# Windowed attention and a gated network: attention from split fp32r products on the full array to plain fp32 products on parts of it

## The chip, the core and the metric

The kernel runs on one core of a Trainium2 chip. The metric is the device time of one execution in microseconds (us), as the median of the runs. TensorE multiplies (its weight loads are listed apart as PEld), VectorE (DVE), ScalarE (ACT) and GpSimd (POOL) work on the memory beside it, and SyncE (SP) issues the copies, which 16 DMA engines carry out.

## The reference

There are 8 batches with 8 heads of width 64. Each batch has 512 local tokens and 32 global ones. A local query sees the 32 global keys and the local keys at a distance of at most 32; a global query sees all 544. All tokens then go through a network with a gate.

```python
s_g = scale * np.matmul(q_g, k_all.transpose(0, 1, 3, 2))
out_g = np.matmul(sm(s_g), v_all)
s_ll = scale * np.matmul(q_l, k_l.transpose(0, 1, 3, 2))
mask = np.abs(pos[:, None] - pos[None, :]) <= window      # window = 32
s_ll = np.where(mask, s_ll, -1000000000.0)
s_lg = scale * np.matmul(q_l, k_g.transpose(0, 1, 3, 2))
a_l = sm(np.concatenate([s_lg, s_ll], axis=-1))
out_l = np.matmul(a_l, np.concatenate([v_g, v_l], axis=2))
...
h = (x @ w1) * (x @ w2) @ w3        # x: 4352 x 512, w1, w2: 512 x 1024, w3: 1024 x 1024
return h @ w_out                     # w_out: 1024 x 512
```

## The kernel before

**The network.** `fold` multiplies w3 with w_out once, at the start, in plain fp32 (64 products of 512 columns). Weights come as 64-bit floats and are brought to fp32 on VectorE and ScalarE (`unit`). Every fp32 number of the network is then held as two fp32r parts, hi and lo, and a product is three: hi x hi, hi x lo, lo x hi. The tokens are cut into 17 keys: 16 half batches of 256 local tokens, and one key of all 256 global ones. A key has four quarters; in a quarter `first` makes 48 products of 256 columns (lines 780 to 782), the gate is multiplied on VectorE, and `second` makes 12 of 512 columns (lines 810 to 812). The gate of a quarter is worked on while TensorE is at the next one.

**Attention.** It goes by heads, and by pairs of heads (32 pairs) where both halves of the partitions are filled. A block has 128 queries and a window of 192 or 256 keys, so a head's scores are four steps (`scores`, line 513). In the first batch (heads under `FS`, `FV` = 8) these are plain fp32 products with 64 rows of contraction (line 506, values at 631 and 634). From the second batch on, keys are stored twice on the partitions (`both_k`, by copies from memory to memory on chip, `KO` and `KE`), so that one product of 128 rows holds q_hi and q_lo against the same keys. VectorE adds the mask and finds the maximum (line 517), ScalarE takes the exponential with its sum (line 521). The weights are turned so that keys stand on partitions: by TensorE's transposes up to head 11, and from head 12 (`FROM`) on by VectorE in blocks of 32 x 32 (line 546) and a way over DRAM (`pd`, then `RT` and `GR`). They are split into hi and lo (`PTh`, `PTl`), multiplied with values (lines 637, 642), and two halves are summed (`cb`, line 659). The inverse of a row's sum goes through DRAM (`rd`) to be laid over 64 partitions (`R`). The global queries of a pair have products of their own (line 691) and transposes (line 730).

**The order.** `ORDER_OF` is a table with one number for each step and, where several engines could do it, a letter for the engine. `in_order` sorts the steps by it, and that is the order on every engine. Each engine works its queue in order; the Tile layer sets the waits between engines.

## Time and profile before

| what | us |
|---|---|
| median of 3 runs | 843.74 |
| lowest, highest | 843.1, 844.06 |
| span of the profiled execution, first to last instruction | 839.6 |
| what lies around it, median of the runs less that span | 4.1 |
| TensorE busy in the span | 822.8 |
| VectorE busy | 669.5 |
| ScalarE busy | 436.8 |
| GpSimd busy | 318.4 |

The profile is of one execution; its own time is given as the span alone. Busy times of TensorE rest on modelled ends, so starts are the better guide there. A record is one line of the trace; several records can belong to one instruction of the program.

### The profile page before, as it was taken

The page shows a single profiled execution, that of the slowest core. Times are in us where ns is not written, and L with a number is a line of the kernel's source. Part 1 is how long each engine was busy: PE and PEld are TensorE (multiplying, and loading weights), DVE is VectorE, ACT ScalarE, POOL GpSimd, SP SyncE. Part 2 cuts the span into 40 slices and gives each one's busy share as a digit, 9 for nine tenths or more (in the row PEclk, how much of TensorE's full clock was granted, in tenths as well). Part 3 has the DMA queues.
Part 4 walks back from the last instruction along what each step waited for, and adds up shares of the span by engine and source line. Part 5 has one row for each costly group of instructions (what it writes and reads, how often), then busy time and mean ns, then how long its engine had stood idle before and what let it go on. Part 6 is the DMA issues. An engine that isn't in the chain of part 4 may idle for free.

```text
span 839.6 us, 17276 instructions
## 1 busy us (share of the span) xinstructions
PE 822.8 (98%) x5694; PEld 732.0 (87%) x5694; DVE 669.5 (80%) x1750; ACT 436.8 (52%) x1230; POOL 318.4 (38%) x465
## 2 busy tenths in 40 slices
PE   7999999799999999999999999999999999999998
PEld 5555469699999989999999999999999999999997
DVE  5878889998888888889898979987989878754343
ACT  5665667855455665467556645565655575400000
POOL 1133245454343634553343545546453555200000
PEclk8999999999999999999999999999999999999999
DMA  7777855566566676676776666667576575410000
GB/s 243 218 251 211 254 136 149 151 167 173 142 167 175 159 176 179 184 173 166 174 190 163 167 167 187 173 156 208 145 183 173 135 190 139 131 34 26 1 26 26
DMA packets 105921, 131.57 MB, mean 157 GB/s; under 512 B 29416, under 2 KB 64232, under 8 KB 105832
## 3 DMA queue, kind: packets, MB, share of 16 engines
q1 hardware_dynamic: 105832, 130.47, 58.5%
q8 instruction: 45, 0.74, 0.4%
q14 instruction: 44, 0.36, 0.2%
HBM read 76.38 MB, written 26.61 MB: 123 GB/s over the span
## 4 chain that ended last, share of the span: by engine, by line
PE 87%; DVE 7%; issue 2%; DMA 2%; ACT 1%; SPq 0%; POOL 0%; DVEq 0%; POOLq 0%; ACTq 0%
PE bp L780 7%; PE w L917 7%; PE bp L781 7%; PE bp L782 7%; PE acc L810 7%; PE ap L780 7%; PE acc L812 7%; PE acc L811 7%; PE ap L781 7%; PE ap L782 7%; PE s L513 5%; PE av L642 5%; PE sg L691 2%; PE av L637 2%; PE av L634 2%
## 5 line engine op out<-in xcount | busy, mean ns | idle before, releaser
L521 ACT ACTIVATE P<-P,mn 128x192 f32<-128x192 f32 (+1 forms) x256 | 121.4, 476 | 72.6 <-DVE mn L517 68.5
L780 PE MATMUL bp<-x,w12h 128*128 128x256 f32 x544 | 152.5, 280 | 1.2 <-DVE gl__8091 L418 1.0
L780 PE MATMUL ap<-x,w12h 128*128 128x256 f32 x544 | 153.0, 281 | 0.0
L781 PE MATMUL bp<-x,w12h 128*128 128x256 f32 x544 | 151.4, 278 | 0.0
L781 PE MATMUL ap<-x,w12h 128*128 128x256 f32 x544 | 151.3, 278 | 0.0
L782 PE MATMUL bp<-x,w12l 128*128 128x256 f32 x544 | 151.3, 278 | 0.0
L782 PE MATMUL ap<-x,w12l 128*128 128x256 f32 x544 | 151.3, 278 | 0.0
L780 PEld LDWEIGHTS bp<-x,w12h 128*128 128x128 f32 x544 | 102.5, 188 | 2.8 <-DVE gl__8091 L418 1.2
L781 PEld LDWEIGHTS ap<-x,w12h 128*128 128x128 f32 x544 | 102.6, 189 | 1.6 <-issue 0.2
L780 PEld LDWEIGHTS ap<-x,w12h 128*128 128x128 f32 x544 | 102.5, 188 | 1.6 <-issue 0.2
L781 PEld LDWEIGHTS bp<-x,w12h 128*128 128x128 f32 x544 | 102.6, 189 | 1.3
L782 PEld LDWEIGHTS ap<-x,w12l 128*128 128x128 f32 x544 | 102.3, 188 | 0.0
L782 PEld LDWEIGHTS bp<-x,w12l 128*128 128x128 f32 x544 | 102.3, 188 | 0.0
L517 DVE CUSTOM_DVE_ANT_0 P<-s,cs 128x192 f32<-128x192 f32 (+1 forms) x256 | 87.9, 385 | 12.4 <-PE s L513 7.6
L659 DVE TENSOR_TENSOR u<-av,cb 64x352 f32<-64x352 f32 x112 | 56.5, 518 | 6.5 <-ACT cb L415 4.6
L917 PE MATMUL w<-wo,w3f 128*128 128x512 f32 x128 | 61.1, 610 | 0.4 <-DVE wo L841 0.4
L415 ACT COPY cb<-av 64x352 f32<-64x352 f32 x95 | 41.7, 447 | 35.1 <-PE av L642 32.8
L546 DVE STREAM_TRANSPOSE P<-P 128x640 f32<-128x640 f32 x52 | 43.7, 841 | 19.0 <-ACT P L521 18.5
L642 PE MATMUL av<-PTl__1026,vs 128*128 128x192 f32 x224 | 55.9, 275 | 0.0
L642 PE MATMUL av<-PTh__1011,vs 128*128 128x192 f32 x224 | 54.5, 268 | 0.1
L521 ACT ACTIVATION_READ_ACCUMULATOR P<-P,mn 128x1 f32 x256 | 48.1, 188 | 0.0
L418 POOL TENSOR_TENSOR PTl__1026<-RT,PTh__1011 128x768 fp32r<-128x768 f32 x19 | 35.6, 1874 | 30.6 <-ACT PTh__1011 L415 15.2
(838 smaller groups left out, 2045.1 us busy)
## 6 DMA issues: line engine op xcount, KB each, us to landing
KO<-KE SPq DMA_DIRECT2D x56, 304.0 KB, 4.2
pd<-P SPq DMA_DIRECT2D x208, 80.0 KB, 2.3
RT<-pd SPq DMA_DIRECT2D x52, 256.0 KB, 3.3
raw_w<-in_w_t_dram SPq DMA_DIRECT2D x24, 512.0 KB, 4.6
kr<-in_kd_t_dram SPq DMA_DIRECT2D x32, 304.0 KB, 4.2
out_dram<-o SPq DMA_DIRECT2D x34, 256.0 KB, 2.6
KE<-KE SPq DMA_DIRECT2D x28, 304.0 KB, 3.3
qr<-in_q_t_dram SPq DMA_DIRECT2D x32, 256.0 KB, 3.7
```

The costliest lines, as they stand in the source:

```text
L517: nc.vector.tensor_tensor_reduce(blk(n, e), cut(n, T["st", n][:, e, 0 : WIN[e][1]]), cut(n, masks[e]), -0.125, 3.0e38, ALU.add, ALU.min, T ...
L521: nc.scalar.activation(blk(n, e), blk(n, e), AF.Exp, bias=T["mn", n][:, e : e + 1], scale=-1.0, accum_out=T["sm", n // 2][:, n % 2, e : e ...
L546: nc.vector.transpose(g[:, 1:6], g[:, 1:6])
L642: nc.tensor.matmul(av[:, o : o + c1 - c0], v, pt[:, j, c0:c1], start=False, stop=(j % 2 == y == 1), skip_group_check=True)
L659: nc.vector.tensor_add(T["u", n // 2][r : r + 64, x], T.pop(("av", n, x))[r : r + 64, 0:352], T["cb", n][r : r + 64, x])
L780: nc.tensor.matmul(d, wh[:, k, c, :], x[:, 0, 0:w], start=(k == m % 2 == 0), stop=False, skip_group_check=True)
L781: nc.tensor.matmul(d, wh[:, k, c, :], x[:, 1, 0:w], start=False, stop=False, skip_group_check=True)
L782: nc.tensor.matmul(d, wl[:, k, c, :], x[:, 0, 0:w], start=False, stop=(k == 3), skip_group_check=True)
L810: nc.tensor.matmul(a, gh[:, m % 2, sl], wh, start=(m == 0), stop=False)
L811: nc.tensor.matmul(a, gh[:, m % 2, sl], wl, start=False, stop=False)
L812: nc.tensor.matmul(a, gl[:, m % 2, sl], wh, start=False, stop=(m == 7))
L917: nc.tensor.matmul(T["w34", t], T["w3f", t, j // 4][:, j % 4], T["wo"][:, j], start=(j == 0), stop=(j == 7))
```

## The change

The network stays as it is: same products, same parts, same gate. Attention is written anew.

- No hi and lo parts of queries, keys, weights and values; products are plain fp32. Keys are not doubled; the sums `cb` and the inverses' way over DRAM are gone, since the result now has queries on partitions and VectorE scales it from the accumulator (`normalize`); four transposes (`back`) bring a pair to the layout of the network.
- A block has 32 queries and a span of 128 keys: 96 local ones (its own 32 and the neighbours) and the 32 global ones. `spread_k` lays a copy of the global keys beside each window in the chip's memory, `load_v` and `spread_v` do the same for values. A block's product has 64 rows and 32 columns of weights in `scores`, and 128 rows and 32 columns in `values`; the partitions of its operands and of its result say which part of the 128 x 128 array it uses.
- From pair 4 (`TP`) on, the weights of both heads of a pair are turned at once (line 349 of the new kernel) and go over DRAM (`Pd`, `Pt`), with five copies. The global queries go the same way (`Gd`, `Gt`).
- The table `ORDER_OF` is new, and so are the pools' sizes.

The core of the diff, with what it calls:

```diff
-        for e in range(4):
-            o, w = WIN[e]
-            for j in range(2):
-                nc.tensor.matmul(st[:, e, 0:w], qs[:, 128 * e : 128 * e + 128], K[:, j, o : o + w],
-                                 start=(j == e % 2 == 0), stop=(j == 1), skip_group_check=True)
+        for g in range(4):
+            for x in range(4):
+                for h in range(2):
+                    c = 128 * g + 32 * x
+                    nc.tensor.matmul(block(st[:, h], x, 128 * g), q[64 * h : 64 * h + 64, c : c + 32],
+                                     window(m, h, 4 * g + x), start=True, stop=True, skip_group_check=True)
...
+    def block(ap, x, c):
+        return ap[32 * x : 32 * x + 32, c : c + 128].rearrange("p (a b) -> p a b", a=2)
...
+    def exps(m, h, g):
+        P = T["P", m][:, :, h, g]
+        nc.scalar.activation(P, P, AF.Exp, bias=T["mn", m][:, g, h : h + 1], scale=-1.0,
+                             accum_out=T["sm", m][:, g, h : h + 1])
...
+    def turned_out(kind, m):
+        P = flat(T[kind, m])
+        d = T[kind + "d", m] = dram.tile([128, 4, 256], F32, tag=kind + "d", name=f"{kind}d{m}", bufs=3)
+        for x in range(4):
+            nc.sync.dma_start(d[:, x].rearrange("(s j) c -> j s c", s=4),
+                              P[32 * x : 32 * x + 32].rearrange("p (s c) -> p s c", s=4))
...
-        nc.tensor.matmul(av[:, g0 : g0 + (256 if x else 288)], vgs.rearrange("p a b -> p (a b)"), G, start=True,
-                         stop=False, skip_group_check=True)
-        for j, o, c0, c1 in parts:
-            v = T["vs", n // 2][:, n % 2, j].rearrange("p a b -> p (a b)")
-            for y, pt in enumerate((W["PTh"], W["PTl"])):
-                nc.tensor.matmul(av[:, o : o + c1 - c0], v, pt[:, j, c0:c1], start=False, stop=(j % 2 == y == 1),
-                                 skip_group_check=True)
+        for h in range(2):
+            for g in range(4):
+                for x in range(4):
+                    nc.tensor.matmul(vt[32 * x : 32 * x + 32, g, h], t[:, x, h, g], Vs[m % NV][:, x, h, g], start=True,
+                                     stop=True, skip_group_check=True)
...
+        for g in range(2):
+            for x in range(4):
+                for h in range(2):
+                    to = st[32 * x : 32 * x + 32, h, 0:256].rearrange("p (a b g j) -> p g a b j", a=2, b=2, g=2)[:, g]
+                    nc.tensor.matmul(to, T["qg", m // NP][64 * h : 64 * h + 64, m % NP],
+                                     window(m, h, 2 * (4 * g + x) + 1).rearrange("p a (b j) -> p a b j", b=2), start=True, stop=True, skip_group_check=True)
```

**TensorE at the start.** First the queue before, from the values of head 0 to the scores of head 2 (`av`, `s`):

```order
L631 MATMUL av_0_310<-G,vgs 64x288
L634 MATMUL av_0_310<-PTh,vr_199 64x192
L634 MATMUL av_0_310<-PTh,vr_199 64x224
L631 MATMUL av_0_322<-G,vgs 64x256
L634 MATMUL av_0_322<-PTh,vr_199 64x224
L634 MATMUL av_0_322<-PTh,vr_199 64x192
L506 MATMUL s_332<-kr_132,qr_143 128x192
L506 MATMUL s_332<-kr_132,qr_143 128x256 x2
L506 MATMUL s_332<-kr_132,qr_143 128x192
```

Now the queue of the change, at a like place; `t` and `xt` are transposes, `sg` the global scores, `w` the folding:

```order
L365 MATMUL t_0_308<-cs,P_234 128x128 x4
L427 MATMUL sg_316<-K_75,qg_189 32x4x32 x16
L645 MATMUL w_2_344<-wo,w3f_0_336 128x512 x4
L365 MATMUL t_1_355<-cs,P_234 128x128 x4
L329 MATMUL s_362<-K_76,q_224 32x128 x32
L645 MATMUL w_2_344<-wo,w3f_1_360 128x512 x4
L379 MATMUL v_427<-V_77,Pt_338 32x64 x32
L427 MATMUL sg_465<-K_76,qg_189 32x4x32 x16
L365 MATMUL t_0_486<-cs,P_365 128x128 x4
L396 MATMUL xt_493<-cs,vo_483 128x128 x4
L365 MATMUL t_1_500<-cs,P_365 128x128 x4
L645 MATMUL w_3_512<-wo,w3f_0_506 128x512 x4
```

A head's scores were four products of 192 and 256 columns with 128 columns of weights; a pair's are now one row of 32 products with 32 columns of weights and 128 keys each, and its values 32 products of 64 columns.

**TensorE in the middle.** Before, between two stretches of the network (the values of head 28 in two halves, and global scores between them):

```order
L637 MATMUL av_28_4662<-G__1017,vgs__1005 128x288
L642 MATMUL av_28_4662<-PTh__1011,vs_4432 128x192
L642 MATMUL av_28_4662<-PTl__1026,vs_4432 128x192
L642 MATMUL av_28_4662<-PTh__1011,vs_4432 128x224
L642 MATMUL av_28_4662<-PTl__1026,vs_4432 128x224
L691 MATMUL sg_4671<-KE_4556,QG 128x288 x4
L637 MATMUL av_28_4680<-G__1017,vgs__1005 128x256
L642 MATMUL av_28_4680<-PTh__1011,vs_4432 128x224
L642 MATMUL av_28_4680<-PTl__1026,vs_4432 128x224
L642 MATMUL av_28_4680<-PTh__1011,vs_4432 128x192
L642 MATMUL av_28_4680<-PTl__1026,vs_4432 128x192
```

In the change, the values of a pair (`v`) and its way back (`xt`) with products of `second` between them:

```order
L379 MATMUL v_4462<-V_78,Pt_4170 32x64 x32
L538 MATMUL acc_0_0_4055<-w34h_952,gh__4406 128x512
L539 MATMUL acc_0_0_4055<-w34l_953,gh__4406 128x512
L540 MATMUL acc_0_0_4055<-w34h_952,gl__4427 128x512
L538 MATMUL acc_0_128_4056<-w34h_952,gh__4406 128x512
L539 MATMUL acc_0_128_4056<-w34l_953,gh__4406 128x512
L540 MATMUL acc_0_128_4056<-w34h_952,gl__4427 128x512
L396 MATMUL xt_4505<-cs,vo_4503 128x128 x4
L538 MATMUL acc_0_0_4055<-w34h_1082,gh__4406 128x512
L539 MATMUL acc_0_0_4055<-w34l_1083,gh__4406 128x512
L540 MATMUL acc_0_0_4055<-w34h_1082,gl__4427 128x512
```

Eleven rows of full-array products for one head have become one row of 32 for two heads, followed at once by products of the network with 128 x 128 weights; the transposes `xt` come one step of `second` later.

**SyncE in the middle.** Before, one head's turned weights come back (`RT`, `GR`), the next head's go out (`pd`), and an inverse is laid out (`R`):

```order
L554 DMA pd_5344<-P_79 32x5x128 x4
L537 DMA R_5370<-rd_5268 64x512
L395 DMA vr_5387<-in_v_t_dram 128x512
L560 DMA RT_76<-pd_5344 128x512
L561 DMA RT_76<-P_79 32x96
L562 DMA RT_76<-P_79 32x96
L563 DMA GR<-pd_5344 32x512
```

In the change, a pair's turned weights go out (`Pd`, four copies) and come back (`Pt`, one copy):

```order
L355 DMA Pd_5704<-P_5482 32x4x256 x4
L273 DMA K_75<-in_kp_t_dram 128x544
L553 DMA out_dram<-o_0_0_5794 128x512
L553 DMA out_dram<-o_0_128_5798 128x512
L360 DMA Pt_5816<-Pd_5704 128x1024
L270 DMA q_5872<-in_q_t_dram 128x512
L273 DMA K_76<-in_kp_t_dram 128x544
L355 DMA Pd_5971<-P_5821 32x4x256 x4
L360 DMA Pt_6083<-Pd_5971 128x1024
```

The loads of keys and queries and the network's results now stand between a pair's way out and its way back in the same queue; the copies for inverses and the three small copies of each head are gone from it.

## Rows read from the trace of the kernel before

**Rows 1.** The page: summary of TensorE, and the chain that ended last by engine.
```profile
PE 822.8 (98%) x5694; PEld 732.0 (87%) x5694; DVE 669.5 (80%) x1750; ACT 436.8 (52%) x1230; POOL 318.4 (38%) x465
...
PE 87%; DVE 7%; issue 2%; DMA 2%; ACT 1%; SPq 0%; POOL 0%; DVEq 0%; POOLq 0%; ACTq 0%
```

**Rows 2.** Busy time by stretch: span, each engine (instructions), TensorE clock, DMA share, GB/s.
```profile
0.00:121.00 121.00, 116.28 (x433) 64.27 (x434) 93.87 (x264) 77.21 (x213) 32.52 (x56) 0.97 0.71 220
121.00:740.00 619.00, 610.54 (x4574) 578.00 (x4573) 535.79 (x1425) 359.62 (x1017) 285.83 (x410) 1.00 0.65 166
```

**Rows 3.** The same middle stretch, instructions of L782 alone (PE, weight loads).
```profile
121.00:740.00 619.00, 251.90 (x906) 170.36 (x906) 1.00 0.65 166
```

**Rows 4.** The same, instructions of L812 alone.
```profile
121.00:740.00 619.00, 88.29 (x224) 42.11 (x224) 1.00 0.65 166
```

**Rows 5.** TensorE in order of time, middle: start, us, line, out<-in, shape, records.
```profile
399.81 0.28 PE L780 MATMUL bp<-x,w12h 128*128 128x256 f32 x1
...
401.22 1.07 PE L513 MATMUL s<-KO,qs 128*128 128x192 f32 x8
402.13 0.41 PE L810 MATMUL acc<-w34h,gh__5136 128*128 128x512 f32 x1
...
403.53 0.28 PE L780 MATMUL bp<-x,w12h 128*128 128x256 f32 x1
...
404.92 0.28 PE L780 MATMUL ap<-x,w12h 128*128 128x256 f32 x1
```

**Rows 6.** TensorE in order of time, start of the kernel.
```profile
63.35 1.12 PE L917 MATMUL w<-wo,w3f 128*128 128x512 f32 x2
64.41 1.78 PE L506 MATMUL s<-kr,qr 64*128 64x192 f32 x8
66.12 0.66 PE L569 MATMUL t<-cs,P 128*128 128x128 f32 x4
66.61 0.49 PE L572 MATMUL t<-cs,P 128*128 128x128 f32 x3
```

**Rows 7.** Its weight loads in order of time, same place.
```profile
63.35 0.30 PEld L917 LDWEIGHTS w<-wo,w3f 128*128 128x128 f32 x2 [0.28 <-issue]
64.41 1.48 PEld L506 LDWEIGHTS s<-kr,qr 64*128 64x128 f32 x8 [0.76 <-DVE x L418]
...
66.83 0.19 PEld L917 LDWEIGHTS w<-wo,w3f 128*128 128x128 f32 x1
```

**Rows 8.** Weight loads by line and shape: count, busy us, mean ns.
```profile
L506 PEld LDWEIGHTS s<-kr,qr 64*128 64x128 f32 x64 | 10.9, 186 | 5.0 <-DVE mn L517 1.0 <-ACT PTh L415 0.8 <-DVE mg L713 0.8
...
L634 PEld LDWEIGHTS av<-PTh,vr 128*64 128x64 f32 x64 | 7.4, 136 | 7.8 <-issue 5.3 <-DVE mn L517 0.9 <-ACT P L521 0.4
```

**Rows 9.** Tile raw_w: durations in ns, first and last start in us.
```profile
L881 SPq DMA_DIRECT2D raw_w<-in_w_t_dram x24: 327/328/577, 2.1 to 106.0; - x24
```

**Rows 10.** DMA issues by line, count, KB each, median us to landing.
```profile
pd<-P SPq DMA_DIRECT2D x208, 80.0 KB, 2.3
RT<-pd SPq DMA_DIRECT2D x52, 256.0 KB, 3.3
raw_w<-in_w_t_dram SPq DMA_DIRECT2D x24, 512.0 KB, 4.6
...
raw_wo<-in_wo_t_dram SPq DMA_DIRECT2D x8, 512.0 KB, 5.1
```

**Rows 11.** VectorE by line and shape: count, busy us, mean ns.
```profile
L517 DVE CUSTOM_DVE_ANT_0 P<-s,cs 128x256 f32<-128x256 f32 x128 | 49.8, 418 | 0.2
...
L546 DVE STREAM_TRANSPOSE P<-P 128x640 f32<-128x640 f32 x52 | 43.7, 841 | 19.0 <-ACT P L521 18.5
...
L517 DVE DVE_READ_ACCUMULATOR2_ANT mn<- 128x1 f32 x256 | 20.9, 82 | 0.0
```

**Rows 12.** ScalarE by line and shape.
```profile
L521 ACT ACTIVATE P<-P,mn 128x256 f32<-128x256 f32 x128 | 64.2, 502 | 31.7 <-DVE mn L517 30.7
...
L521 ACT ACTIVATION_READ_ACCUMULATOR P<-P,mn 128x1 f32 x256 | 48.1, 188 | 0.0
```

## The prediction

> **What bounds the kernel now.** I read the page first: the summary says TensorE is busy 98% of a span of 839.6 us, and the chain that ended last lies on it for 87% [rows 1]. The chip's rows model the ends of matmuls, so I checked that with starts. Cut into three stretches, the span is a start of 121 us at 116.28 busy, a middle of 619 us at 610.54, and a tail with the gated network alone [rows 2]. In the middle the starts follow each other without a hole: 12 products of `first` take 1.41 us (399.81 to 401.22) and again 1.39 (403.53 to 404.92), so 0.1167 each; six of `second` take 1.40 us, 0.233 each; the scores of one head, between them, 0.91 [rows 5]. The reader is to see a queue that is never empty. [...] So the time of the middle is a sum over TensorE's steps, and only a shorter sum shortens it. VectorE, with 535.79 us of the 619, is next.

> The middle has 906 products at L782, and 2,719 at the three lines of `first` together; 224 at L812, and 672 at the three of `second` [rows 3, 4]. They take 2,719 x 0.1167 + 672 x 0.233 = 474 us. The other 145 us are attention: seven of eight batches, 28 pairs of heads, so **5.18 us a pair**. The change must beat this number. The network's steps are the same before and after, instruction by instruction.

> **The change, part by part.**

> *What a plain fp32 product costs.* The start of the kernel has some. The scores of a head there are four products of 192, 256, 256 and 192 columns, and the trace holds eight records of them, two to a product [rows 6]. They start at 64.41, the next step at 66.12. [...] So 128 columns cost 0.213 us as two records of 0.107, and 64 columns 0.107 as two of 0.053, if nothing runs beside them. That the contraction has 64 rows gives no discount.

> *What a pair asks for now.* Scores: 32 products of 128 columns. Values: 32 of 64. Global scores: 16 of 128. Global values: 32 of 64 for two pairs. One after the other that is 6.83 + 3.41 + 3.41 + 1.71 = 15.4 us. Scores stand on eight places of the array (two groups of rows, four of columns), values on four. If all places work at once it is 0.85 + 0.85 + 0.43 + 0.43 = 2.56 us. No row of before has two products at work on different places, so these are the bounds.

> *The way back to 512 tokens* is four transposes a pair; four of them take 0.49 us from 66.12 to 66.61, the first one's load among it, so 0.11 each [rows 6], so 0.44, and 0.05 for the global one.

> *Changing the shape.* At 63.35 two records of L917 start, full array: a load of 0.107 and 2 x 0.427 of stream end at 64.31, and the scores' load starts at 64.41 only; in the unbroken queue a load starts while the product before streams, as L917's does at 66.83 [rows 6, 7]. So a new shape costs 0.10 us and lays its first load open. Loads of 128 and of 64 columns differ by 0.050 us in duration [rows 8], so I take 0.107 for 128 and, scaled, 0.027 for 32 columns. The new order changes shape 198 times, 112 times to a small one and 86 times back: 112 x 0.127 + 86 x 0.207 = 32 us, 1.0 a pair. [...]

> So a pair costs between 2.56 + 0.49 + 1.0 = **4.05** and 15.4 + 0.49 + 1.0 = **16.9 us**. The nearest row for work side by side is that load under a running product: places that hold other weights need not wait for each other there. I take the lower end and add 0.1 for each of 3.5 steps, since a step's first records cannot all start at one instant: **4.4 us**. Over 28 pairs this is 28 x 0.78 = 22 us less. [...]

> *The start.* Before, TensorE is full for 121 us: 128 records of L917 with 0.43 each are 55, the rest is attention of the first batch in fp32. Now 55 of folding stay, and four to five pairs come to some 20 us, with a warm-up about 78. Then the weights set the pace: 32 pieces were fetched from 2.1 to 106.0 us, one every 3.35, and land in 4.6 [rows 9, 10]. The network's first product needs 28 of them: 2.1 + 27 x 3.35 + 4.6 + 2 for unpacking = 99 us, where it started at 120.5. That is **21.5 us less**. Bounds: 90, if pieces come faster now that VectorE and the queues have less beside them; 121, if the first batch's attention ends as late as before.

> *VectorE, ScalarE.* A maximum over 128 columns costs at most what one over 256 does, 418 + 82 ns for its read, and an exponential at most 502 + 188 ns; there are 256 of each, as before [rows 11, 12]. A transpose of 1,024 columns is 1.6 x 841 ns = 1.35 us; 44 of them are 59 us, where 52 over 640 columns alone took 43.7. The splits of weights, keys and values into two parts go. So VectorE has no more to do than its 535.79 us of 619, and nothing of this is gained or paid by itself: TensorE hides it. SyncE issues fewer copies; the doubled keys and the broadcast inverses are gone.

> *The turn over DRAM.* Values now wait for 0.9 (scores) + 0.5 + 8 x 0.69 (eight exponentials behind the first maximum) + 1.35 (transpose) + 1 (four issues) + 2.3 and 3.3 (landings as of `pd` and `RT` [rows 10]) = 15 us. Where the new order is tightest it leaves eight `first` and four `second` with small steps between, 20 us. So it is hidden, by 5 us; behind a late one TensorE's whole queue would stand.

> **Sum**, against the profile's own span: 839.6 - 21.5 - 22 = 796; the runs' median lies 4.1 us above the span, so **800 us**. With 4.05 a pair and a start of 90 it is 781, with 5.0 a pair and a start of 108 it is 826. Break-even is 5.18 + 21.5/28 = 5.95 us a pair.

> **Rivals.**
> *Pairs of records block each other* (slower). A product's two records stand on the same place and follow each other in the queue. If products start strictly in order, the second record waits for the first, and the next place waits behind both: only one record's overlap is left, so each product costs one record: 32 x 0.107 + 32 x 0.053 + 16 x 0.107 + 16 x 0.053 = 7.7 us, 9.2 a pair, 28 x 4.0 = 113 more: **935 us**. For it: in all rows products start in order. Against it: nothing in the rows yet shows that a place waits for another one. [...] It decides from 5.95 us a pair.
> *Loads in single file* (slower). Loads of 32 columns, 0.027 each and one at a time, make 196 records a pair 5.2 us, 6.7 a pair: 843.7 - 21.5 + 43 = **865 us**. For it: the two loads at 63.35 take 0.30 us together and one alone 0.19, so they start 0.11 apart [rows 7]. Against it: those go to the same columns.
> *No overlap* (the change does not do what it says): 16.9 a pair, +328, and no earlier start: **1,170 us**.
> *The turn ends last*: if both landings took three times as long under load, 15 would be 26, and the tight half of the pairs 6 us late: 800 + 14 x 6 = **884 us**; from 3.1 us late on each it is no gain. Against it: `pd` and `RT` landed at these medians while the queues moved as much.

> **How the numbers follow.** Overlap as summed 66%, single-file loads 14%, blocked pairs 13%, no overlap 4%, late turn 3%. The first is nearly all faster (0.64), with a little from the second and the last; 0.2% is about what a measurement of this kernel can tell from no change, and almost no case lies so near: same 0.02; slower 0.32. The likeliest's own range is 776 to 826. The range for 8 in 10 takes in single-file loads and the late turn, from 768 to 885, and leaves out blocked pairs and no overlap, 17%, with 2% below.

> **What would show it.** In the profile after: scores of a pair at 1.0 to 1.2 us from the first record's start to the next full-array load, with records of different places starting a few ns to 30 ns apart. Starts 0.107 apart mean blocked pairs; 0.027 apart all through, single-file loads; 0.21 a product, no overlap. The network's first product stands near 99 us. A gap ahead of the values, ended by the DMA of `Pt`, would be the late turn. The forecast is wrong if a pair costs over 5.95 us, or if the start stays at 120.

## The result, and the profile after

The changed kernel takes **808.19 us** (median of 4 runs, 807.36 to 809.57) where the kernel before took 843.57 (4 runs on the same chip, 843.1 to 844.06): the ratio is 0.9585, 95% interval 0.9571 to 0.9598, so 35.4 us less. The profiled spans are 839.6 and 807.1 us, 32.5 apart.

The page of the changed kernel, TensorE's line of the summary and the chain that ended last, as in [rows 1]:

```profile
PE 777.9 (96%) x10676; PEld 670.9 (83%) x10676; DVE 413.0 (51%) x1333; ACT 324.0 (40%) x970; POOL 55.2 (7%) x88
...
PE 89%; DVE 4%; DMA 3%; ACT 2%; issue 1%; SPq 0%; DVEq 0%; ACTq 0%
```

Nearly twice as many TensorE instructions take 45 us less, and the chain stays on TensorE. VectorE, ScalarE and GpSimd lost 256, 113 and 263 us of work, and little of that can show in the time by itself: VectorE had 7% of the chain before and has 4% now. Busy time by stretch (columns as in [rows 2]):

```profile
0.00:102.00 102.00, 86.47 (x972) 44.65 (x973) 64.41 (x210) 57.81 (x159) 14.81 (x38) 0.95 0.79 241
102.00:150.00 48.00, 38.94 (x460) 34.24 (x459) 38.79 (x109) 20.43 (x58) 8.60 (x12) 0.86 0.69 198
150.00:240.00 90.00, 89.84 (x1421) 80.60 (x1419) 51.62 (x177) 38.64 (x124) 6.38 (x8) 1.00 0.55 155
240.00:657.40 417.40, 416.45 (x6413) 375.99 (x6411) 215.12 (x741) 176.60 (x560) 24.34 (x30) 1.00 0.54 154
657.40:807.10 149.70, 146.14 (x1420) 135.46 (x1418) 43.09 (x100) 30.52 (x70) 1.04 (x1) 1.00 0.21 61
```

The second row is the one to remember: 9.1 us of holes on TensorE, and a clock of 0.86, in the first 48 us of the network. From 150 to 657 us the queue is full.

**A pair in the steady part.** The same stretch of 417.4 us holds this many instructions of one of the three lines of `first`, and of one of `second` (columns as in [rows 3, 4]):

```profile
240.00:657.40 417.40, 177.66 (x640) 120.69 (x640) 1.00 0.54 154
```

```profile
240.00:657.40 417.40, 63.06 (x161) 30.05 (x160) 1.00 0.54 154
```

and, grouped by line, the scores of 20 pairs (1,280 records, 64 a pair):

```profile
L329 PE MATMUL s<-K,q 64*32 64x128 f32 x1280 | 23.1, 274 | 0.0
```

So 1,920 x 0.1167 + 480 x 0.233 = 336 us are the network's, and the other 81.5 are 20 pairs: **4.08 us a pair**, worked out as the 5.18 of before was. Both take 0.1167 and 0.233 us for a product of the network. Where one such product directly follows another, starts are in fact 0.1148 and 0.2298 us apart on average here, and 0.1154 and 0.2319 in the middle of before; with these a pair is 4.34 us and was 5.34, so the gain is 1.0 to 1.1 us a pair.

**One step of scores**, TensorE in order of time (compare the middle of [rows 5]):

```profile
398.71 0.28 PE L510 MATMUL ap<-x,w12l 128*128 128x256 f32 x1
398.92 1.16 PE L329 MATMUL s<-K,q 64*32 64x128 f32 x64
400.00 0.38 PE L508 MATMUL bp<-x,w12h 128*128 128x256 f32 x1
400.23 0.28 PE L509 MATMUL bp<-x,w12h 128*128 128x256 f32 x1
```

From the end of the last full product's share (398.71 + 0.117) to the next full product are 1.17 us; one after the other the 32 products, with two records of 0.109 us each as the starts below show them, would need 7.0. The single records of this step start at these times (ns within the span, from the trace; 64 in all):

```
398919 398925 398932 398939 398945 398952 398959 398965
399052 399059 399065 399072 399079 399085 399092 399099
399161 399168 399175 399181 399188 399195 399201 399208
399270 ...
399707 399714 399723 399740 399757 399773 399790 399806
```

Eight records start 7 ns apart. The next eight follow 0.133 us after the first, and from then on a row starts every 0.109. In the last four rows the later records are some 16 ns apart (the last row is shown), so this step lasts 0.05 us longer than its streams alone. Read from the spacing, a row is one record on each of the eight places; eight rows of 0.109 are 0.87 us.

**The first product of the network**, TensorE in order of time, is at 102.15 us (120.56 before):

```profile
101.39 1.11 PE L396 MATMUL xt<-cs,vo 128*128 128x128 f32 x4 [0.78 <-DVE vo L389]
102.15 0.56 PE L508 MATMUL ap<-x,w12h 128*128 128x256 f32 x1
```

From there to the last `first` it is 695.6 us, 709.7 before; the tail is as long as it was. So 18.4 came from the start and 14.1 from the middle. What TensorE waited for between 102 and 150 us (engine, line, releaser: us in total, times, longest):

```profile
PE bp L508 <- DVE gl__1520 L402: 3.4, 1, 3.4
PE ap L508 <- DVE w12h L399: 1.9, 1, 1.9
PE bp L508 <- DVE gl__1258 L402: 1.3, 1, 1.3
PE bp L508 <- DVE gl__1652 L402: 0.7, 1, 0.7
PE ap L509 <- DVE x L402: 0.6, 1, 0.6
PE ap L510 <- POOL w12l L402: 0.6, 2, 0.3
PE ap L508 <- ACT w12h L399: 0.6, 1, 0.6
```

and busy time in the stretch behind the first of these waits (its clock is the third number from the end of the row):

```profile
121.00:128.60 7.60, 4.71 (x88) 3.97 (x76) 6.24 (x17) 4.45 (x14) 0.59 (x1) 1.00 0.61 178
128.60:132.00 3.40, 2.94 (x13) 2.97 (x14) 3.12 (x8) 1.00 (x3) 0.00 (x0) 0.50 0.72 180
132.00:142.30 10.30, 7.50 (x47) 6.32 (x46) 7.53 (x22) 3.49 (x8) 2.31 (x4) 1.00 0.71 202
142.30:149.10 6.80, 5.78 (x80) 4.77 (x79) 5.33 (x19) 2.92 (x10) 0.80 (x2) 0.50 0.40 133
```

The first wait lasted 3.35 us, until 129.06:

```profile
129.06 0.55 PE L508 MATMUL bp<-x,w12h 128*128 128x256 f32 x1 [3.35 <-DVE gl__1520 L402]
```

In its last 0.4 us the granted clock fell to 0.50, where it stayed for 3.4 us: the products of `first` from 129.41 to 131.55 start 0.214 us apart. Behind the waits around 140 us it stayed there for 6.8. It had been there as the network began, too:

```profile
101.30:104.70 3.40, 3.25 (x14) 2.95 (x14) 3.39 (x4) 1.59 (x5) 1.03 (x1) 0.50 1.03 260
```

The kernel before had a granted clock of 1.00 all through its middle [rows 2].

### The profile page after: what moved, and what is told of

Its sections match the earlier page's. It is cut to its first block, busy times and chain, and to the rows that moved or that the text cites. A ratio compares the mean times of both kernels' runs of the same rounds, so it can differ in the third digit from the quotient of the medians.

```text
span 807.1 us, 25268 instructions
## 1 busy us (share of the span) xinstructions
PE 777.9 (96%) x10676; PEld 670.9 (83%) x10676; DVE 413.0 (51%) x1333; ACT 324.0 (40%) x970; POOL 55.2 (7%) x88
## 4 chain that ended last, share of the span: by engine, by line
PE 89%; DVE 4%; DMA 3%; ACT 2%; issue 1%; SPq 0%; DVEq 0%; ACTq 0%
PE acc L538 8%; PE bp L508 8%; PE acc L540 8%; PE acc L539 8%; PE ap L508 8%; PE bp L510 7%; PE bp L509 7%; PE ap L509 7%; PE ap L510 7%; PE w L645 5%; PE s L329 4%; PE v L379 4%; PE sg L427 2%; PE gx L462 2%; PE xt L396 2%; DMA raw_wo<-in_wo_t_dram 1%
## 5 line engine op out<-in xcount | busy, mean ns | idle before, releaser
L508 PE MATMUL bp<-x,w12h 128*128 128x256 f32 x512 | 148.4, 290 | 5.3 <-DVE gl__1520 L402 3.4
L508 PE MATMUL ap<-x,w12h 128*128 128x256 f32 x512 | 145.2, 284 | 2.5 <-DVE w12h L399 1.9
L509 PE MATMUL ap<-x,w12h 128*128 128x256 f32 x512 | 142.9, 279 | 0.6 <-DVE x L402 0.6
L509 PE MATMUL bp<-x,w12h 128*128 128x256 f32 x512 | 143.1, 280 | 0.0
L341 ACT ACTIVATE P<-P,mn 128x128 f32<-128x128 f32 x256 | 99.8, 392 | 27.5 <-DVE mn L336 26.7
L336 DVE CUSTOM_DVE_ANT_0 P<-s,cs 128x128 f32<-128x128 f32 x256 | 58.8, 285 | 66.3 <-PE s L329 60.7
L645 PEld LDWEIGHTS w<-wo,w3f 128*128 128x128 f32 x128 | 23.6, 199 | 40.4 <-issue 21.6
L305 POOL COPY K<-K 128x480 f32<-128x480 f32 x28 | 16.8, 603 | 399.5 <-DMA K<-in_kp_t_dram 378.5
L545 ACT COPY o<-acc 128x512 f32<-128x512 f32 x34 | 20.0, 587 | 52.6 <-PE acc L540 51.1
L295 ACT COPY V<-vg 32x1024 f32<-32x1024 f32 x33 | 33.7, 1045 | 16.1 <-PE gx L465 15.9
L399 ACT CAST x<-xt 128x256 fp32r<-128x256 f32 x50 | 17.6, 373 | 55.0 <-PE xt L396 53.5
L379 PEld LDWEIGHTS v<-V,Pt 128*32 128x32 f32 x2048 | 30.2, 110 | 10.1 <-issue 4.1
```

Of the source, the lines that this page charges most:

```text
L295: (nc.scalar.copy if eng is nc.scalar else eng.tensor_copy)(to, src)
L336: nc.vector.tensor_tensor_reduce(T["P", m][:, :, h, g], chunks(T["s", m][:, h, 128 * g : 128 * g + 128]), chunks(masks[g]), -0.125, 3.0e38 ...
L341: nc.scalar.activation(P, P, AF.Exp, bias=T["mn", m][:, g, h : h + 1], scale=-1.0, accum_out=T["sm", m][:, g, h : h + 1])
L379: nc.tensor.matmul(vt[32 * x : 32 * x + 32, g, h], t[:, x, h, g], Vs[m % NV][:, x, h, g], start=True, stop=True, skip_group_check=True)
L508: nc.tensor.matmul(d, wh[:, k, c, :], x[:, 0, 0:w], start=(k == m % 2 == 0), stop=False, skip_group_check=True)
L509: nc.tensor.matmul(d, wh[:, k, c, :], x[:, 1, 0:w], start=False, stop=False, skip_group_check=True)
```

## The experiments

Each was timed beside the kernel before on the same chip; times are medians, ratios are to the kernel before, and the changed kernel's own is 0.9585.

### Two places at a time

```diff
-        for g in range(4):
-            for x in range(4):
+        for x in range(4):
+            for g in range(4):
                 for h in range(2):
```

> The same 32 products of a scores step, ordered so that only two places of the array (the two groups of rows) alternate, each with four products one behind the other. Theory (places work at once, but records start in the order of the queue): 16 rounds of 0.213 us are 3.41 where eight places took 0.85, so a step grows from 1.11 to about 3.7 us, 28 steps in the middle add 72 us and the four of the start up to 10 more: 880 to 890 us. Rival A (each place has a queue of its own, so order does not matter): 808. Rival B (the gain came from the new order around the network and from lighter other engines, not from places side by side): within 5 of 808.

Measured: 850.61 us, ratio 1.0074 (1.0043 to 1.0106), 0.7% above the kernel before. TensorE, the same step:

```profile
400.69 2.48 PE L329 MATMUL s<-K,q 64*32 64x128 f32 x64
```

Neither number came: a step grew to 2.48 us, not 3.7 and not 1.11. The records told why; the first of them start at these times (ns, as above):

```
400686 400692 400819 400826 400928 400935 401037 401044 401146 401153 401159 401166
```

The two places of one x start a record every 0.109 us (the second 0.133 after the first), but the two places of the next x do not wait for the last of these. They start 0.473 us after the first two, just behind their fifth record. So the order matters (2.48 us a step here, 1.16 in the change), and these records do not start in strict order of the queue. Rival B falls too: the order of these 32 products alone, with the rest of the kernel kept, costs 42 us, more than the whole gain of 35.4.

### One place at a time

```diff
-        for g in range(4):
-            for x in range(4):
-                for h in range(2):
+        for x in range(4):
+            for h in range(2):
+                for g in range(4):
```

> The 32 products of a scores step ordered so that each of the eight places gets its four products in a row. Theory formed from the order with two places (a place's records wait for their own place alone, and the queue can run ahead until three records wait at a place, so the next place starts when the fifth of eight records starts, 0.47 us after the last one did): a step takes 7 x 0.473 + 1.06 = 4.4 us in place of 1.11, 28 to 32 steps: 899 to 913 us. Rival A (records start strictly in the order of the queue): 8 x 0.87 = 7.0 us a step, 973 to 996. Rival B (a queue without end at each place): 808.

Measured: 909.60 us, ratio 1.0777 (1.0754 to 1.0801), where the theory said 899 to 913. TensorE, the same step:

```profile
455.25 4.32 PE L329 MATMUL s<-K,q 64*32 64x128 f32 x64
```

Its first records start at these times (ns):

```
455252 455386 455495 455604 455713 455719 455822 455852
```

The first place's records keep their 0.109 behind a first interval of 0.134; the second place's first one (455719) starts 6 ns behind the fifth (455713), and its second 0.133 later at 455852, while the first place goes on at 455822. Rival A would have given 7.0 us a step; even without any time between places, strict order needs 8 x 7 x 0.109 = 6.1. The same 32 products cost 1.16, 2.48 or 4.32 us by their order alone. That records belong to this or that place is read from their spacing; the trace does not name places.

### More columns, as many records

```diff
+                    if g < 3:
+                        to = st[32 * x : 32 * x + 32, h, 128 * g : 128 * g + 256]
+                        to = to.rearrange("p (r a b) -> p r a b", r=2, a=2)
+                        keys = keys.unsqueeze(1).to_broadcast([64, 2, 2, 64])
...
```

> 24 of the 32 products of a scores step stream 256 columns instead of 128, the second half being overwritten by the next product; as many records and as many loads as before. Theory (a step lasts as long as the columns that one place streams): 3 more streams of 0.213 a place, 0.64 us a step, so 18 us over the 28 steps of the middle and up to 2.5 in the start: 826 to 829 us. Rival (a step lasts as long as 64 records need to be issued, or their weights to be loaded, one after the other, 17 ns each): 808, and steps still 1.11 us.

Measured: 828.54 us, ratio 0.9811 (0.9784 to 0.9839), and the step:

```profile
410.09 1.74 PE L334 MATMUL s<-K,q 64*32 64x256 f32 x64
```

0.58 us more a step, near the 0.64 of the theory. With 24 of the 32 products twice as wide, a place streams seven times 128 columns instead of four, and the step took 1.74 us instead of 1.16. Issuing 64 records and loading weights 64 times cost the change's step some 0.05 us, by an estimate from its last row: here the last row's eight records start 7 ns apart again (46 ns from first to last), where they took 99 ns in the change.

### Scores cut in two

Between the halves stands one step of `first`; from the fifth pair on.

```diff
+        rest.append(m) if m >= TP else None
+        some_scores(m, range(4 if m < TP else 2))
...
+            if rest and k[0] == "first" and SPLIT:
+                some_scores(rest.pop(), range(2, 4))
```

> Each scores step from the fifth pair on is cut in two halves with one step of the network between them: 27 more changes to a small shape and back, the same products. By the forecast's price (0.127 and 0.207 us) it is +9.0: 817 us. By the rows of the changed kernel (of a step's 1.11 us only 0.85 is stream, and the products around a step lose some 0.19 more) +27 x 0.45 = 12: 820 us. If a change of shape cost nothing: 808.

Measured: 815.58 us, ratio 0.9658 (0.9631 to 0.9686), 7.4 more than the change (6.2 by the ratios), so about a quarter of a microsecond, 0.27, for each of 27 more stretches of a small shape. The two intervals together leave 2.6 us either way, 0.1 for each stretch, so the forecast's 0.334 is not ruled out, and no cost at all is. A half, TensorE in order of time:

```profile
400.61 0.28 PE L517 MATMUL ap<-x,w12l 128*128 128x256 f32 x1
400.82 0.67 PE L336 MATMUL s<-K,q 64*32 64x128 f32 x32
401.41 0.39 PE L515 MATMUL bp<-x,w12h 128*128 128x256 f32 x1
401.64 0.28 PE L516 MATMUL bp<-x,w12h 128*128 128x256 f32 x1
```

Half the products leave 0.68 us of the 1.17, where half the stream is 0.43: some 0.25 us of a step are not stream, and the full product behind it takes 0.23 instead of 0.117.

### Small steps side by side

Twelve small steps are renumbered, with the steps that hang on them, to stand beside another one: 74 stretches in place of 86.

```diff
-    v="... 1205 1250 ..."    vg="... 1276 ..."
+    v="... 1225.5 1250 ..."  vg="... 1250.5 ..."
```

> Twelve small steps are moved beside another small step (values of pairs 9, 13, 17, 21, 25, 29 behind scores; global values of six pairs of pairs behind values), so there are 74 stretches of small shapes in place of 86, with the same products. By what the split of the scores cost (7.4 us for 27 more stretches, 0.27 each): -3.3, 805 us. By the forecast's 0.334: -4.0, 804. If the price of a stretch came from the scores being cut and not from the change of shape: 808.

Measured: 809.48 us, ratio 0.9582 (0.9568 to 0.9595): no change, which is the third of the numbers named, so this run does not bear out a price for each stretch. Two things in the traces may explain it. A step of values behind scores is still a change of shape (64 x 32 to 128 x 32), so only part of the price goes: in the changed kernel's trace the two take 2.21 us side by side and 1.18 and 1.12 apart (medians of 11, 14 and 9 of them from 150 us on), with one slow full product behind them instead of two. And this run's trace has two holes, 1.6 and 1.0 us, in which TensorE waited for nothing that the profile shows (`issue`), and 0.7 for a copy of V:

```profile
PE gx L370 <- issue: 1.6, 1, 1.6
PE gx L373 <- issue: 1.0, 1, 1.0
PE v L287 <- DMA V<-in_v_t_dram: 0.7, 1, 0.7
```

Whether the holes belong to this order, and whether gathering steps pays without them, stays open.

### The turn left out

From the fifth pair on nothing is transposed or sent to DRAM for the probabilities.

```diff
     def turn(kind, m):
+        if kind == "P":
+            return
...
```

> From the fifth pair on the turn of the probabilities is left out (VectorE's transpose, four copies to DRAM and one back): the values read the unturned probabilities, so the output is another one. Theory (the turn is hidden behind TensorE, in the middle only TensorE's sum counts): 0 to -4 us, what there is coming from 100 to 150 us, where TensorE does wait. Rival (the turn's end, or VectorE's and the queues' load, sets part of the middle): -10 or more.

Measured: 808.03 us, ratio 0.9570 (0.9547 to 0.9594). The turn is hidden, and some 35 us of VectorE's time (28 x 1.24) are free.

### Fewer folds

```diff
+        if t < 2 or j % 2 == 0 or j == 7:
             nc.tensor.matmul(T["w34", t], T["w3f", t, j // 4][:, j % 4], T["wo"][:, j], start=(j == 0), stop=(j == 7))
```

> 18 of the 64 fp32 products that fold the third weights are left out (0.854 us each, 15.4 us of TensorE's work before the network starts), so those weights are wrong; all weights are still fetched and unpacked. By the forecast's step (the weights' pace sets the start of the network) the first product of the network stays at 99 to 102 us and the time at 805 to 808. Rival (from 28 us on TensorE's own work sets it): the first product near 87 to 92 us; how much of it reaches the end is open, since the next weights are then waited for: 795 to 807.

Measured: 799.56 us, ratio 0.9467 (0.9449 to 0.9484). TensorE in order of time:

```profile
90.16 0.56 PE L508 MATMUL ap<-x,w12h 128*128 128x256 f32 x1
```

The first product comes 12.0 us earlier for 15.4 us less of folding. The 28th piece, which the forecast waited for, is fetched earlier too; SyncE's issue of it in the changed kernel, and here:

```profile
89.47 0.33 SPq L609 DMA_DIRECT2D raw_w<-in_w_t_dram  x1
```

```profile
78.14 0.33 SPq L609 DMA_DIRECT2D raw_w<-in_w_t_dram  x1
```

So here the pieces follow the folding, not the folding the pieces. Of the 12.0 us, 4.8 are lost again before the 193rd product.

### The stretch from 102 to 150 us

The low part of the gated values earlier in VectorE's queue (two numbers):

```diff
-    gl="458 533 592 651 ..."
+    gl="458 511.5 570.5 651 ..."
```

> The second and the third quarter's low part of the gated values are put straight behind their high part in VectorE's queue, ahead of the unpacking and splitting of weights that stood before them. Theory (TensorE's waits at 125.3 and 142.7 us come from VectorE's order, and each is followed by half the clock): 3.4 + 0.7 us of waits and up to 5 us of half clock go, -4 to -9: 799 to 804 us. Rival (the weights of the second half land and are split at a pace of their own, the network waits for them in any order): 806 to 808, with a longer wait for w12h further on.

Less unpacking (of the small pieces, steps 0 and 3):

```diff
+        if kind == "w12s" and step in (0, 3):
+            return
```

> For the 16 small pieces of the second half of the first weights, two of the steps of unpacking (VectorE's shift and its merge, 0.287 and 0.481 us each) are left out, so those weights are wrong. Theory (between 102 and 150 us VectorE's work on weights holds up the network): some 10 of its 38.8 us in that stretch go, the waits (9 us) and the half clock behind them go for the most part: 795 to 801 us. Rival (the DMA of the weights sets that stretch, or the clock falls for another reason): 805 or more.

Fewer fetches:

```diff
+        if kind == "w12s" and e:
+            T[kind, a, e] = T[kind, a, 0]
+            return
```

> Of the 16 small pieces of the second half of the first weights only the first of each four is fetched; the other 12 unpack and split the same buffer again (wrong weights), with all of VectorE's, ScalarE's and GpSimd's work kept. Theory (between 102 and 150 us the pieces' pace through a ring of three buffers, 5.8 us of landing each, holds up the network, so neither VectorE's order nor a lighter VectorE helped much): the waits of some 12 us there and the half clock behind them shrink by half or more, 798 to 803 us. Rival (the work of unpacking sets the pace): 806 or more, with the same waits.

All three (the first and the third edit, and no unpacking where nothing is fetched):

```diff
+        if kind == "w12s" and e and step < 4:
+            return
```

> Three reliefs at once for the stretch from 102 to 150 us: of the 16 small pieces only every fourth is fetched and unpacked (the others split the same buffer, wrong weights, no waiting for one another), and the low parts of the gated values stand early in VectorE's queue. Theory (landing, VectorE's work on the pieces and VectorE's order are about equally late there, so that taking one away uncovers the next): the waits of 11 to 12 us and the half clock behind them go for the larger part, 796 to 801 us. Rival (what is waited for is none of the three): 805 or more.

| kernel | us | ratio (95%) | first product | 193rd product | between | from there to the last `first` |
|---|---|---|---|---|---|---|
| the change | 808.19 | 0.9585 (0.9571 to 0.9598) | 102.2 | 154.5 | 52.4 | 643.2 |
| low part early | 808.92 | 0.9577 (0.9561 to 0.9593) | 100.2 | 155.6 | 55.4 | 642.2 |
| less unpacking | 804.10 | 0.9524 (0.9510 to 0.9537) | 100.8 | 151.7 | 50.9 | 642.0 |
| fewer fetches | 808.24 | 0.9578 (0.9560 to 0.9596) | 100.6 | 152.9 | 52.3 | 642.9 |
| all three | 801.77 | 0.9477 (0.9431 to 0.9523) | 101.9 | 147.5 | 45.6 | 643.5 |

(Starts of products of `first`, in us of the profiled span.) The first alone only moved the wait: TensorE's waits from 98 to 150 us with the low part early,

```profile
PE ap L508 <- DVE w12h L399: 6.6, 2, 3.6
PE ap L508 <- ACT w12h L399: 2.8, 1, 2.8
PE bp L508 <- DVE gl__1258 L402: 1.5, 1, 1.5
```

name the weights' high parts with 9.4 us, and `gl` with 1.5 where it had 5.4. Less unpacking won 4.1 us in all but only 1.4 of them in the stretch, fewer fetches nothing (there the 12 pieces shared a buffer and so waited for each other, which blurs it; and the 5.8 us of landing in its theory are of the first three pieces, while the 13 of this stretch landed in 3.5). All three won 6.8 in the stretch, and the busy time of 102 to 150 us shows where:

```profile
102.00:150.00 48.00, 43.12 (x574) 38.77 (x572) 37.41 (x108) 19.48 (x62) 8.97 (x12) 0.93 0.53 159
```

4.9 us of holes instead of 9.1, a clock of 0.93 instead of 0.86. The theory had said 796 to 801 and got 801.77, whose interval is wide; the stretch itself fits it: several suppliers about equally late, each hiding behind the next. That is not shown, though: for 12 of the 16 pieces this run leaves out the whole unpacking, ScalarE's step too, and no run left that out alone.

### Splits moved off VectorE

```diff
-    unit="... D482 D487 ... D514 ... D539 D540 ..."
+    unit="... A482 P487 ... A514 ... A539 P540 ..."
```

> Of the small pieces' splits in two, ten casts go from VectorE to ScalarE and four subtractions from VectorE to GpSimd, by letters in the table alone. If VectorE's load between 102 and 150 us is part of what the network waits for, as the lighter unpacking let it appear (-4 us for 12 us less): some 6 us less on VectorE give -1 to -2, 806 to 807 us. If the pieces' landing or the clock sets it, or the slower subtraction ends last: 808 to 810.

In the edit nine casts and six subtractions moved, not ten and four. Measured: 806.98 us, ratio 0.9560 (0.9544 to 0.9575), 1 to 2 us below the change (1.2 by the medians, 2.1 by the ratios), as expected, but the intervals overlap: not told apart from it. It has the lowest median of the versions with the whole computation.

## Why the prediction was right, and where it was off

Forecast 800 us, in the likeliest case's range of 776 to 826; measured 808.19. The mechanism was right: places side by side make attention's sum on TensorE shorter. Of the two terms, -21.5 and -22, the spans show -18.4 and -14.1.

**What a pair costs** was forecast at 4.4 us and is 4.08, or 4.34 by the spacing that the network's products show. The places work at once, as taken (1.16 us for a step of scores, where one after the other would be 7.0). No row or run shows the 0.213 us for 128 columns from which the forecast's sums are made: in the step of before at 64.41 us, records of 256 columns start 0.216 us apart, so that two records of 128 are 0.216 (these have 64 rows of contraction; the transposes behind them, with 128 rows and 128 columns, start 0.109 apart), and in the change a place's records of 128 columns start 0.109 apart, two of them 0.218. The 0.1 us a step for starts one behind the other was too much, since the first eight records of the step at 398.92 start within 0.05. The changes of shape were forecast at 1.0 us a pair, 0.334 for a stretch; splitting the scores priced a stretch at 0.27, with 0.1 either way.

**"28 x 0.78 = 22 us less" is the step that failed.** With the pair as measured it would even be 28 x 1.0 to 1.1, so 28 to 31. But the sum took the middle to be without holes however early it begins. Between 102 and 150 us TensorE lost 9.1 us in holes and, at half the clock in 101.3 to 104.7, 128.6 to 132.0 and 142.3 to 149.1, some 5.5 of its busy time: about 15 us, where 14 to 17 are missing between these 28 to 31 and 14.1. The network starts 18.4 us earlier, and what it waits for there are the gates' low parts (5.4 us) and the second half of its first weights (3.1), made for the most part in VectorE's queue. The kernel before had holes too, but 8.5 us of them in all 619 of its middle [rows 2], and those are in its 5.18. All three reliefs together took back 6.8 us; which of them did it, and what the rest waits for, stays open.

**The start** came out at 102 where 99 was forecast, by a wrong reason, so that it came out so near is luck. "Then the weights set the pace" fell with the fewer folds. TensorE itself, with folding and attention, is busy from 28 to 92 us with hardly a break, and the pieces' buffers come free as it folds:

```profile
28.00:92.00 64.00, 62.02 (x784) 32.07 (x787) 43.82 (x154) 38.46 (x117) 3.63 (x6) 0.99 0.79 240
```

From 92.25 to 99.2 the chain lies for the most part on ScalarE (copies of values, exponentials), then on a pair's values and its way back. TensorE was 86.47 us busy before the first product, not 78.

**The turn** is hidden, as forecast. **VectorE** has less work than bounded: 286 ns for a maximum of 128 columns, 1.24 us for a transpose, and leaving the turn out gave nothing where TensorE is full.

**The rivals.** Loads in single file and no overlap fell with starts 7 ns apart. "Pairs of records block each other" fell too, and its premise, that records start strictly in the order of the queue, was wrong as such: with one place at a time a step would have taken 6.1 us at the least and took 4.32. The record at 455719, taken for the second place's first, starts between those at 455713 and 455822, taken for the first place's fifth and sixth. So an engine that works its queue in order is not what the starts of TensorE's records show here.

## What to carry to other kernels

Products on parts of the array paid here only where neighbours in the queue stood on different places: with eight places in turn a step took 1.16 us, with two 2.48, with one at a time 4.32, and the kernels 808.19, 850.61 and 909.60 us. Do not cut such a step in two without need: each further stretch cost 0.27 us here, with 0.1 either way. That gathering steps of different small shapes gains this back is not shown; here it gained nothing. When a change lets a stage begin earlier, ask what that stage eats in its first microseconds and whether this, too, comes earlier; here 9.1 us of holes, and some 5.5 us lost at a granted clock of 0.50, took back part of the gain.
